# Fill products in the tensor engine's waits at the end of part A, and one in place of six ahead of the second B chunk

## The chip, the cores and the metric

The kernel runs on one core of a Trainium2 chip. The metric is device time in microseconds (us) of one execution. TensorE (PE) does the products, VectorE (DVE) and ScalarE (ACT) the copies and the softmax, GpSimd (POOL) copies inside SBUF and passes semaphores on, SyncE (SP) issues nearly all DMA transfers.

## The reference

Two attention decode steps with one query per batch row, put side by side in the output. Part A has 32 query heads on 8 key/value heads and looks only at the last 2048 positions. Part B has 32 heads of its own and looks at all 8192.

```
q = (x @ wq) -> [4, 32, 1, 128]
A: k, v = cache[:, :, Sk - W:, :], each shared by 4 heads;   W = 2048
B: k, v = cache, whole;                                      Sk = 8192
p = softmax(q . k * 128**-0.5);  o = (p . v) @ wo
out = concat([A, B], axis=-1)                # 4 x 1 x 1024, bf16
```

Nearly all the bytes are the B caches: 4 x 32 x 8192 x 128 values of two bytes, twice, which is 537 MB of the 587 MB that are read.

## The kernel before

Work is cut into chunks. Part A has 8 chunks (`NCA`), one for each key/value head, with 2 MB of keys and 2 MB of values each. Part B has 32 chunks, four heads of one batch row each, with 8 MB of keys and 8 MB of values.

Keys arrive with positions on partitions, so PE transposes them in tiles of 128 x 128, eight tiles a group, into the PSUM tile `tr` (`emit_T`, recorded at L499). DVE or ACT copies a group to `kt` (L572, L570), and PE forms the scores of a group with products of up to 64 columns into `sc` (`emit_S`; nearly all plain products are recorded at L501). After the statistics and the exponentials, PE multiplies the weights with the values into `po` and, for the second half of a B chunk, into a part of `tr` (`emit_pv`). The output projection accumulates in `fin`.

Each engine runs a list of operations in a fixed order, written out by the code; waits are on counters of the other engines. SP's list is the order of the transfers: wq, the A chunks, then for each B chunk k and v (a B k transfer is issued at L408, a B v transfer at L447, A's keys and values at L378). A transfer waits until the place it writes is free: k of the next chunk until the transposes of the first half of this chunk's keys are done, v until the products of the chunk before have read their half of the values. POOL passes the landing of each B transfer on to PE (`land_kB`, `land_vB`) and copies the second half of each k into a spare place (L423), which starts when that k has landed.

The end of part A is `finish_A`. It works off what is left of the last A chunk, on PE in this order: the transpose of the row maxima (`gmax-1`), four small products that sort the outputs of the chunk before (`sel-2`), the broadcast of the maxima (`bc-1`), the 128 products that form part B's queries (`q_products(1)`), the sum for the norm (`norm-1`), 64 products with the last A values (`emit_pv`), and again four small products (`emit_sel`).

A B chunk is `whole_B`. On PE it begins with `reorder` (16 products of 512 columns on 32 rows), two products whose result nobody reads (`keep_busy`, `NBUSY = 2`), and `more_busy`, a loop of such products at L927: `MOREBUSY + 1 = 6` in the chunks 1 to 28 of part B and one in the chunks 0, 29, 30 and 31. The first groups of transposes come after it. Such products without a use are called fill products here. Another helper, `fill(n)` (L944), loops over n of them; it stands twice at the start of the kernel (`FILL = (6, 3)`), before and after the products that form part A's queries. Its moving operand is a part of `pba` that holds zeros, and it waits for POOL to have written `identb` and `pba`.

The lists of PE, DVE and ACT are searched for repeating stretches, and these are written as loops; `finish_A` lies outside them.

Of the kernel before, what the change touches and what calls it, by code (L numbers as in the profile page):

```python
# [34 lines left out]
MOREBUSY = 5  # L35
# [141 lines left out]
def bass_concat_heads__sliding_block_cached__mha_block_cached__decode_kernel(  # L177
# [6 lines left out]
    DO = A_wo.shape[1]  # L184
# [37 lines left out]
    sch = _Sched()  # L222
    with ExitStack() as es:
        block = es.enter_context(nc.Block())

        def sb(name, shape, dt):
            return es.enter_context(nc.sbuf_tensor(name, shape, dt))

        def ps(name, shape, dt):
            return es.enter_context(nc.psum_tensor(name, shape, dt))  # L230
# [10 lines left out]
        identb = sb("identb", [P, P], BF16)  # L241
# [23 lines left out]
        pbt = {0: sb("pba", [P, NPB, NTA * 16 + NW], BF16), 1: sb("pbb", [P, 2, NTB * 2 + NW], BF16)}  # L265
# [4 lines left out]
        sel4 = sb("sel4", [P, 4, P], BF16)  # L270
# [5 lines left out]
        sc = ps("sc", [P, 2, 512], F32)  # L276
# [15 lines left out]
            fill=0.0, base=0, channel_multiplier=-1), waits=["c_onesb"], key="c_identb")  # L292
# [4 lines left out]
            fill=0.0, base=0, channel_multiplier=-1), waits=["c_onesf"], key="c_identf")  # L297
# [4 lines left out]
            waits=["c_onesf", "c_identf"], key="c_ind")  # L302
# [14 lines left out]
        for r in range(4):  # L317
            sch.add("pool", lambda e, r=r: e.affine_select(
                out=sel4[:, r, :], in_=onesb[:, :], pattern=[[0, 4], [-4, 32]], compare_op=ALU.is_equal,
                fill=0.0, base=-r, channel_multiplier=1), waits=["c_onesb"], key="c_sel" if r == 3 else None)  # L320
# [3 lines left out]
        for u in range(4):  # L324
            sch.add("pool", lambda e, u=u: e.affine_select(
                out=back[:, :, :], in_=back[:, :, :], pattern=[[1, 4], [-1, P]], compare_op=ALU.not_equal,
                fill=1.0, base=-P * u, channel_multiplier=4), waits=["c_back0" if u == 0 else ("c_back", u - 1)], key=("c_back", u))
# [14 lines left out]
        def flat(at, n):  # L342
            return kv[:, at:at + n, :].rearrange("p s x -> p (s x)")
# [153 lines left out]
        def pe_mm(o, l, r, start=True, stop=True, transpose=False, waits=(), key=None):  # L497
            if transpose:
                sch.add("pe", lambda e: e.transpose(o, l, r), waits, key)  # L499
            else:  # L500
                sch.add("pe", lambda e: e.matmul(o, l, r, start=start, stop=stop), waits, key)  # L501
# [13 lines left out]
        def q_products(ab):  # L515
            wqr = flat(half_of[("wq", ab)], 2)
            for h in range(HQ):
                for r in range(KC):
                    last = h == HQ - 1 and r == KC - 1
                    pe_mm(ms[:, Q0 + h * NB: Q0 + (h + 1) * NB], wqr[:, (r * HQ + h) * P:(r * HQ + h + 1) * P],  # L520
                          xT[:, ab, r * NB:(r + 1) * NB], start=r == 0, stop=r == KC - 1,
                          waits=[("wq", ab), "xT"] + ms_read if h == r == 0 else [],
                          key=("qmm", ab) if last else None)

        def q_out(ab):
            src = ms[:, Q0:Q0 + HQ * NB]
            dst = qs[:, ab * NB * HQ:(ab + 1) * NB * HQ]
            if ab == 1:

                src, dst = src.rearrange("p (hq u b) -> p hq b u", b=NB, u=4), dst.rearrange("p (hq b u) -> p hq b u", b=NB, u=4)  # L530
            else:
                src, dst = src.rearrange("p (g c b) -> p g b c", b=NB, c=REP), dst.rearrange("p (g b c) -> p g b c", b=NB, c=REP)
            sch.add("dve", lambda e: e.tensor_copy(dst, src), waits=[("qmm", ab), "c_qs"], key=("q", ab))
            ms_read[:] = [("q", ab)]
# [206 lines left out]
        def emit_pv(c, g):  # L741
            ch = chunks[c]
            UC = ch["UC"]
            half = NTB // 2
            for t in range(TG):
                j = g * TG + t
                if c < NCA:
                    base = 16 * (c % NSM)
                    waits = [("exp", c)] + po_read + [("v", c)] if j == 0 else []
                    if j == 0:  # L750
                        po_read[:] = []
                    pe_mm(po[:, base:base + NW], tile_of("v", c, j), pbt[0][:, par(c), j * UC:j * UC + NW],
                          start=j == 0, stop=j == ch["NT"] - 1, waits=waits, key=("pv", c) if j == ch["NT"] - 1 else None)
                    continue
                h, jj = j // half, j % half
                waits = [("exp", c, h)] + (po_read if h == 0 else []) if jj == 0 else []
                if j == 0:
                    po_read[:] = []
                waits += [("vr", c, g)] if t == 0 and g in QV else []
                o = (po2 if h else po)[:, 0:NW]  # L760
                pe_mm(o, tile_of("v", c, j), pbt[1][:, h, jj * 4:jj * 4 + NW], start=jj == 0, stop=jj == half - 1,
                      waits=waits, key=("pv", c, h) if jj == half - 1 else None)
# [35 lines left out]
        def norm_out(c):  # L798
            if c < NCA:
                m = c % NSM  # L800
                o, i0, i1 = oT[:, m, :], po[:, m * 16:m * 16 + 16], rinv[:, m, :]
                waits = [("rinv", c), ("pv", c)] + ([("sm", c - 2)] if c >= 2 else [])
            else:

                o, i0 = oz[:, :].rearrange("p (b u) -> p b u", b=NB), bcast(po2[:, 0:4], [[0, NB], [1, 4]])
                i1 = rz[:, :].rearrange("p (b u) -> p b u", b=NB)
                waits = [("rz", c), ("pv", c, 1)] + ([("fin", c - 1)] if c > NCA else ["c_oz"])
            sch.add("dve", lambda e: e.tensor_tensor(out=o, in0=i0, in1=i1, op=ALU.mult), waits=waits, key=("oT", c))
            if c < NCA:
                po_read[:] = [("oT", c)]  # L810
# [14 lines left out]
        def reord_at(u):  # L825
            return po[:, :] if u == 3 else tr[:, u, :].bitcast(F32)
# [51 lines left out]
        def do_A(what, c):  # L878
            name, n = what.split("-")
            c -= int(n)  # L880
            if c < 0:
                return
            {"gmax": stats_gmax, "bc": stats_bc, "shift": shift_A, "exp": exp_A, "sums": sums_A, "norm": norm_sum,
             "spread": lambda c: spread_A(c, range(4)), "spread01": lambda c: spread_A(c, (0, 1)), "spread23": lambda c: spread_A(c, (2, 3)),
             "sel": emit_sel, "fin": emit_fin}[name](c)
# [36 lines left out]
        def more_busy(c):  # L922

            n = c - NCA

            def mm(e):
                return e.matmul(sc[:, 1, :], identb[:, :], sel4[:, :, :].rearrange("p r x -> p (r x)"), start=True, stop=True)  # L927

            def emit(e, x=0):
                if isinstance(e, _Record):  # L930
                    return mm(e)
                if isinstance(x, int):
                    mm(e)
                    return None
                with nc.Fori(0, (((x + n + 31) >> 5) - ((x + n + 3) >> 5)) * MOREBUSY + 1, 1, engines=type(mybir.ALL_ENGINES)([mybir.EngineType.PE])):
                    mm(e)
                return None

            sch.add("pe", emit, at=n)

        def fill(n):

            def mm(e):
                return e.matmul(sc[:, 1, :], identb[:, :], pbt[0][:, 1, 0:DO], start=True, stop=True)  # L944

            def emit(e):
                if isinstance(e, _Record):
                    return mm(e)
                with nc.Fori(0, n, 1, engines=type(mybir.ALL_ENGINES)([mybir.EngineType.PE])):
                    mm(e)  # L950
                return None

            sch.add("pe", emit, waits=["c_identb", ("c_pb", 0)])

        def whole_B(c):

# [41 lines left out]
            emit_fin(c)  # L998

        def finish_A():  # L1000
            for what in ['gmax-1', 'sel-2', 'bc-1', 'shift-1', 'exp-1']:
                do_A(what, NCA)
            q_products(1)
            for what in ['spread-1', 'sums-1']:
                do_A(what, NCA)
            q_out(1)
            sch.relay("act", sems, "eng_sp", 1, [("q", 1)])
            do_A('norm-1', NCA)
            for g in range(chunks[NCA - 1]["NG"]):
                emit_pv(NCA - 1, g)  # L1010
            norm_out(NCA - 1)
            emit_sel(NCA - 1)

        emit_xT()
        fill(FILL[0])
        q_products(0)
        q_out(0)
        fill(FILL[1])
        emit_qb(0)
        for c in range(NCA):  # L1020
# [3 lines left out]
            values_A(c - 1 if c else None, c)  # L1024
        sch.mark()
        finish_A()
        for c in range(NCA, NC):
            whole_B(c)
# [67 lines left out]
```

## Time and profile before

| | us |
|---|---|
| median of 3 runs | 1373.03 (1371.73 to 1373.15) |
| the profiled execution, its own time | 1370.3 |
| its span, first to last instruction | 1368.6 |
| PE busy | 1230.5 (90%) |
| PE weight loads busy | 1125.3 (82%) |
| DVE busy | 731.5 (53%) |
| ACT busy | 555.5 (41%) |
| POOL busy | 210.1 (15%) |
| mean granted TensorE clock | 0.974 |

All times inside an execution count from the start of its span. A row of the timeline gives the start, the length, engine, line, operation, the tiles (out<-in) and the number of instructions; in square brackets stands how long the engine was idle before the row and what ended that. A row of the windows view gives for a stretch its length, then busy time and count for PE, PE's weight loads, DVE, ACT and POOL, then the granted TensorE clock (1.00 is full), the busy share of the 16 DMA engines and the GB/s they moved. A share a little over 1 in a short stretch comes from whole packets being counted in it.

### The profile page before, as it was taken

Reading aid. Unit: us, or ns where it says so; the run is one execution under the profiler, and the core shown is the slowest. Engines: PE = TensorE matmul, PEld = TensorE weight load, DVE = VectorE, ACT = ScalarE, POOL = GpSimd, SP = SyncE. Lnnn points to the kernel's source line nnn. Section 1 sums busy time; section 2 is a strip of 40 time slices with the busy share of each in tenths; the row PEclk is TensorE's granted clock in tenths of the full one; section 3 lists DMA queues with packets and bytes.
Section 4 is the critical chain, followed back from the end, with each engine's and each line's share of the span. In section 5 each row is a group of like instructions: output and inputs, shape, how many; then the busy total and the mean of one; then the engine's idle time right before and its main releaser. Section 6 shows DMA issues by size and latency. Waiting matters only on the chain.

```text
span 1368.6 us, 62991 instructions
## 1 busy us (share of the span) xinstructions
PE 1230.5 (90%) x27848; PEld 1125.3 (82%) x27848; DVE 731.5 (53%) x1495; ACT 555.5 (41%) x777; POOL 210.1 (15%) x86
## 2 busy tenths in 40 slices
PE   6868799988988999989989999898999898989998
PEld 5767688888887988878889888888888888878888
DVE  3655355554554555545545555454555554546555
ACT  3533244433444443434344434333444343434444
POOL 2000022222210222222101222221012222210000
PEclk9988999999999999999999999999999999999999
DMA  9999999999999999999999999999999999999998
GB/s 399 429 426 429 432 435 431 425 433 429 429 437 437 429 429 431 442 429 429 439 433 431 431 435 441 439 421 433 444 433 423 437 439 435 429 433 435 420 432 349
DMA packets 16053, 587.52 MB, mean 429 GB/s; under 512 B 1800, under 2 KB 1824, under 8 KB 3872
## 3 DMA queue, kind: packets, MB, share of 16 engines
q1 hardware_dynamic: 16000, 587.21, 99.6%
q8 instruction: 15, 0.25, 0.1%
q14 instruction: 6, 0.05, 0.0%
q10 hardware_dynamic: 32, 0.01, 0.0%
HBM read 587.21 MB, written 0.01 MB: 429 GB/s over the span
## 4 chain that ended last, share of the span: by engine, by line
DMA 50%; PE 44%; issue 2%; DVE 2%; ACT 1%; ACTq 0%; SPq 0%; POOLq 0%; DVEq 0%
DMA kv<-in_B_k_cache_dram 47%; PE tr L499 24%; PE sc L501 11%; PE tr L501 4%; DMA kv<-in_A_k_cache_dram 3%; PE po L501 2%; PE ms L501 1%; DMA kv<-in_A_wq_dram 1%; PE sc L927 1%; PE fin L501 1%; DVE kt L572 1%; ACT pbb L694 1%; DVE sA L625 0%; PE ms L499 0%; ACT pba L724 0%
## 5 line engine op out<-in xcount | busy, mean ns | idle before, releaser
L499 PE MATMUL tr<-identb,kv 128*128 128x128 bf16 x8704 | 670.7, 223 | 47.8 <-POOLq L80 35.3
L572 DVE COPY kt<-tr 128x1024 bf16<-128x1024 bf16 x736 | 502.5, 690 | 319.9 <-PE tr L499 316.5
L499 PEld LDWEIGHTS tr<-identb,kv 128*128 128x128 bf16 x8704 | 520.0, 100 | 60.5 <-issue 46.5
L570 ACT ACTIVATE kt<-tr 128x1024 bf16<-128x1024 bf16 x352 | 359.6, 1024 | 457.8 <-PE tr L499 455.6
L501 PE MATMUL sc<-qq,kt 128*128 128x64 bf16 x8192 | 400.9, 192 | 11.3 <-DVE kt L572 9.4
L423 POOL COPY kv<-kv 128x4096 int32<-128x4096 int32 x56 | 200.2, 3604 | 1021.1 <-DMA kv<-in_B_k_cache_dram 1021.1
L501 PEld LDWEIGHTS sc<-qq,kt 128*128 128x128 bf16 x8192 | 330.7, 98 | 17.9 <-DVE kt L572 12.7
L694 ACT ACTIVATE pbb<-sc,negb 32x128 bf16<-32x128 f32 x256 | 138.1, 540 | 133.6 <-DVE negb L676 130.8
L501 PE MATMUL tr<-pbb,kv 128*128 128x64 bf16 x4096 | 135.6, 193 | 29.0 <-ACT pbb L694 25.6
L501 PEld LDWEIGHTS tr<-pbb,kv 128*128 128x128 bf16 x4096 | 131.0, 99 | 32.7 <-issue 32.7
L501 PE MATMUL po<-pbb,kv 128*128 128x64 bf16 x4096 | 133.8, 193 | 1.0 <-issue 1.0
L501 PEld LDWEIGHTS po<-pbb,kv 128*128 128x128 bf16 x4096 | 126.3, 98 | 2.1 <-issue 1.1
L842 ACT ACTIVATE wol<-tr 128x512 bf16<-128x512 f32 x32 | 19.1, 597 | 202.2 <-PE po L501 202.2
L844 DVE CAST wol<-tr 128x512 bf16<-128x512 f32 x64 | 41.2, 685 | 56.1 <-PE tr L501 53.2
L927 PE MATMUL sc<-sel,identb 128*128 128x512 bf16 x172 | 53.3, 390 | 13.8 <-issue 13.8
L927 PEld LDWEIGHTS sc<-sel,identb 128*128 128x128 bf16 x172 | 17.0, 99 | 50.6 <-issue 40.7
L701 DVE TENSOR_REDUCE rs<-pbb 128x4 f32<-128x512 bf16 x32 | 21.9, 686 | 50.3 <-ACT pbb L694 50.3
L501 PE MATMUL tr<-wos,back 32*128 32x512 bf16 x384 | 35.7, 390 | 0.7 <-issue 0.5
L774 DVE RECIPROCAL ib<-ms 128x8 f32<-128x8 f32 x32 | 6.6, 208 | 53.3 <-PE ms L501 53.3
L501 PE MATMUL po<-wos,back 32*128 32x512 bf16 x128 | 34.7, 392 | 0.0
L662 DVE TENSOR_REDUCE gm<-ms 4x4 f32<-4x128 f32 x72 | 19.8, 274 | 25.2 <-PE ms L499 25.2
L642 DVE TENSOR_REDUCE rh<-sc 128x4 f32<-128x512 f32 x32 | 22.1, 691 | 14.3 <-PE sc L501 14.3
(90 smaller groups left out, 515.9 us busy)
## 6 DMA issues: line engine op xcount, KB each, us to landing
kv<-in_B_v_cache_dram SPq DMA_DIRECT2D x9, 4096.0 KB, 22.1
kv<-in_B_k_cache_dram SPq DMA_DIRECT2D x6, 4096.0 KB, 19.8
kv<-in_A_k_cache_dram SPq DMA_DIRECT2D x8, 2048.0 KB, 15.3
kv<-in_A_v_cache_dram SPq DMA_DIRECT2D x8, 2048.0 KB, 16.0
kv<-in_B_k_cache_dram SPq DMA_DIRECT2D x4, 2048.0 KB, 22.4
kv<-in_A_wq_dram SPq DMA_DIRECT2D x1, 4096.0 KB, 12.6
wor<-in_A_wo_dram SPq DMA_DIRECT2D x8, 512.0 KB, 22.1
kv<-in_B_wq_dram SPq DMA_DIRECT2D x1, 4096.0 KB, 17.4
```

What stands on the lines that cost most here:

```text
L423: sch.add("pool", lambda e, dst=dst, org=org: e.tensor_copy(dst, org), waits=[("T", s0 + ch["NG"] - 1)] if g == QC[0] else [])
L499: sch.add("pe", lambda e: e.transpose(o, l, r), waits, key)
L501: sch.add("pe", lambda e: e.matmul(o, l, r, start=start, stop=stop), waits, key)
L570: sch.add("act", lambda e: e.activation(dst, src, ACTF.Copy), waits=waits, key=("ev", s))
L572: sch.add("dve", lambda e: e.tensor_copy(dst, src), waits=waits, key=("ev", s))
L642: sch.add("dve", lambda e: e.tensor_reduce(out=dst, in_=src, axis=AX.X, op=ALU.max), waits=[("S", ch["s"] + (half + 1) * ch["NG"] // 2 - 1 ...
L662: sch.add("dve", lambda e: e.tensor_reduce(out=gm[0:C, m, 0:U], in_=src, axis=AX.X, op=ALU.max), waits=[key_of("trm", c, half)], key=key_o ...
L694: sch.add("act", lambda e, src=src, dst=dst, pp=pp, u=u: e.activation(dst, src, ACTF.Exp, bias=negb[pp, half, u:u + 1], scale=scale), wait ...
L701: sch.add("dve", lambda e: e.tensor_reduce(out=dst, in_=probs_of(c, half).rearrange("p j u -> p u j"), axis=AX.X, op=ALU.add), waits=[("ex ...
L842: sch.add("act", lambda e, u=u, o=o: e.activation(wol[:, u, :], o, ACTF.Copy), waits=[("reord", c, u)], key=("wol", c, u))
L844: sch.add("dve", lambda e, u=u, o=o: e.tensor_copy(wol[:, u, :], o), waits=[("reord", c, u)], key=("wol", c, u))
L927: return e.matmul(sc[:, 1, :], identb[:, :], sel4[:, :, :].rearrange("p r x -> p (r x)"), start=True, stop=True)
```

## The change

Three things change.

- `finish_A` gets four fill products in three loops: two ahead of `gmax-1`, one ahead of `bc-1`, and one between `q_products(1)` and the sum for the norm. They write `reord_at(0)`, the first bank of `tr`.
- `more_busy` runs one fill product in place of six in chunk 1, the second B chunk. All other chunks keep their number.
- `fill` takes an output as a second argument, and its moving operand is now `sel4`, the selection matrix that `more_busy` streams too; it waits for `sel4` instead of `pba`. This holds for the two old places as well.

```
-                with nc.Fori(0, (((x + n + 31) >> 5) - ((x + n + 3) >> 5)) * MOREBUSY + 1, 1, ...):
+                with nc.Fori(0, (((x + n + 30) >> 5) - ((x + n + 3) >> 5)) * MOREBUSY + 1, 1, ...):
                     mm(e)
...
-        def fill(n):
+        def fill(n, at=None):
             def mm(e):
-                return e.matmul(sc[:, 1, :], identb[:, :], pbt[0][:, 1, 0:DO], start=True, stop=True)
+                return e.matmul(sc[:, 1, :] if at is None else at, identb[:, :],
+                                sel4[:, :, :].rearrange("p r x -> p (r x)"), start=True, stop=True)
...
-            sch.add("pe", emit, waits=["c_identb", ("c_pb", 0)])
+            sch.add("pe", emit, waits=["c_identb", "c_sel"])
...
         def finish_A():
-            for what in ['gmax-1', 'sel-2', 'bc-1', 'shift-1', 'exp-1']:
+            for n, what in zip((2, 0, 1, 0, 0), ('gmax-1', 'sel-2', 'bc-1', 'shift-1', 'exp-1')):
+                if n:
+                    fill(n, reord_at(0))
                 do_A(what, NCA)
             q_products(1)
+            fill(1, reord_at(0))
             for what in ['spread-1', 'sums-1']:
                 do_A(what, NCA)
```

More of the change, by code (lines that the diff above doesn't have):

```diff
@@ L934, in emit @@
                     return None
-                with nc.Fori(0, (((x + n + 31) >> 5) - ((x + n + 3) >> 5)) * MOREBUSY + 1, 1, engines=type(mybir.ALL_ENGINES)([mybir.EngineType.PE])):
+                with nc.Fori(0, (((x + n + 30) >> 5) - ((x + n + 3) >> 5)) * MOREBUSY + 1, 1, engines=type(mybir.ALL_ENGINES)([mybir.EngineType.PE])):
                     mm(e)
@@ L939, in more_busy @@
             sch.add("pe", emit, at=n)
-        def fill(n):
+        def fill(n, at=None):
             def mm(e):
-                return e.matmul(sc[:, 1, :], identb[:, :], pbt[0][:, 1, 0:DO], start=True, stop=True)
+                return e.matmul(sc[:, 1, :] if at is None else at, identb[:, :], sel4[:, :, :].rearrange("p r x -> p (r x)"), start=True, stop=True)
             def emit(e):
```

## The prediction

> **What bounds the kernel now.** I read the page first: the row of DMA shares, the bytes and the chain that ended last.
>
> ```profile
> span 1368.6 us, 62991 instructions
> ...
> DMA  9999999999999999999999999999999999999998
> ...
> HBM read 587.21 MB, written 0.01 MB: 429 GB/s over the span
> ...
> DMA 50%; PE 44%; issue 2%; DVE 2%; ACT 1%; ACTq 0%; SPq 0%; POOLq 0%; DVEq 0%
> ```
>
> The transfers fill the span. PE takes nearly half of the chain as well, so the question is whether PE ever makes a transfer start too late. POOL's timeline answers it, because its first copy in a chunk starts when that chunk's k has landed and PE has finished the chunk before.
>
> ```profile
> 171.57 7.14 POOL L423 COPY kv<-kv 128x4096 int32<-128x4096 int32 x2 [160.06 <-DMA kv<-in_B_k_cache_dram]
> 210.32 7.15 POOL L423 COPY kv<-kv 128x4096 int32<-128x4096 int32 x2 [31.61 <-DMA kv<-in_B_k_cache_dram]
> 249.09 7.15 POOL L423 COPY kv<-kv 128x4096 int32<-128x4096 int32 x2 [31.62 <-DMA kv<-in_B_k_cache_dram]
> 289.07 7.15 POOL L423 COPY kv<-kv 128x4096 int32<-128x4096 int32 x2 [32.83 <-DMA kv<-in_B_k_cache_dram]
> 327.79 7.15 POOL L423 COPY kv<-kv 128x4096 int32<-128x4096 int32 x2 [31.56 <-DMA kv<-in_B_k_cache_dram]
> ```
>
> The k of B chunks 1 to 5 land 38.75, 38.77, 39.98 and 38.72 us apart. Between two stand 16.78 MB (8 MB of v, 8 MB of k; the third distance also holds 0.52 MB of wo, 1.2 us). That is 433 MB per ms each time. The first distances, where PE is still late, are as short as the last, where PE waits for the data. So from 171.57 us on the transfers lose nothing to PE. SP's timeline shows why: each transfer is issued before the one ahead of it has landed.
>
> ```profile
> 122.11 0.80 SPq L447 DMA_DIRECT2D kv<-in_B_v_cache_dram  x2
> ...
> 160.79 8.56 SPq L447 DMA_DIRECT2D kv<-in_B_v_cache_dram  x2
> 185.53 0.33 SPq L408 DMA_DIRECT2D kv<-in_B_k_cache_dram  x1
> 202.29 5.49 SPq L447 DMA_DIRECT2D kv<-in_B_v_cache_dram  x2
> ...
> 244.76 0.33 SPq L447 DMA_DIRECT2D kv<-in_B_v_cache_dram  x1
> ```
>
> 8 MB take 38.72 / 2 = 19.4 us. Slack, landing ahead minus issue: v of chunk 0, 171.57 - 38.7 - 122.11 = 10.8; first half of v 1, 171.57 - 160.79 = 10.8; k 2, 171.57 + 19.4 - 185.53 = 5.4; v 2, 210.32 - 202.29 = 8.0; v 3, 249.09 - 244.76 = 4.3. The least is 4.3 us. PE may be later than now by that much before the end moves, and being earlier moves nothing behind 171.57.
>
> What can be won lies ahead of it. The last A chunk's k landed at 87.20 + 13.26 = 100.46.
>
> ```profile
> 87.20 13.26 DMA kv<-in_A_k_cache_dram
> ```
>
> From there to 171.57 are 71.1 us for two A v (2.1 MB each), 0.52 MB of wo and three 8 MB transfers, 29.9 MB, which at the steady 433 take 69.0. So 2.1 us at most are lost there, to whatever cause, and this is the ceiling of any gain through earlier transfers in this execution.
>
> **The change part by part.** PE at the end of part A and at the start of part B:
>
> ```profile
> 108.57 1.56 PE L501 MATMUL po<-pba,kv 128*128 128x64 bf16 x48
> ...
> 111.49 0.27 PE L499 MATMUL ms<-identf,rm 128*4 128x128 f32 x1 [1.35 <-DVE rm L637]
> ...
> 113.20 0.58 PE L501 MATMUL ms<-identf,gx 4*128 4x4 f32 x2 [0.81 <-DVE zA L821]
> ...
> 114.13 3.55 PE L501 MATMUL ms<-xT,kv 128*128 128x4 bf16 x128 [0.35 <-DVE negb L680]
> ...
> 118.06 0.60 PE L501 MATMUL ms<-rsa,onesf 128*128 128x16 f32 x2 [0.38 <-DVE qs L533]
> ...
> 118.51 3.57 PE L501 MATMUL po<-pba,kv 128*128 128x64 bf16 x64
> ...
> 123.19 0.63 PE L501 MATMUL tr<-wos,back 32*128 32x512 bf16 x3 [0.50 <-issue]
> ...
> 126.31 1.77 PE L499 MATMUL tr<-identb,kv 128*128 128x128 bf16 x24
> ```
>
> *The four fills.* A fill of the same shape runs in the kernel now:
>
> ```profile
> 172.95 2.30 PE L927 MATMUL sc<-sel,identb 128*128 128x512 bf16 x6
> ...
> 175.09 1.50 PE L499 MATMUL tr<-identb,kv 128*128 128x128 bf16 x24
> ```
>
> Six from 172.95 to 175.09 are 0.36 us each. Two stand in the 1.35 us wait for the row maximum (0.72, fits), one in the 0.81 us wait ahead of `bc` (fits), one in the 0.38 us wait ahead of the norm (0.36; at worst it pushes the 64 value products by its own length). Nothing queued behind them is late; I cost them at 0 (between 0 and 0.4 us on PE). If the idle time went away they would cost 4 x 0.36 = 1.4 us of PE, within the slack.
>
> *What the fills may do: the clock.* The windows view, cut into stretches of 3.41 us that end at the falls and rises of the granted clock:
>
> ```profile
> 109.79:113.20 3.41, 0.87 (x17) 0.47 (x13) 2.95 (x11) 0.00 (x0) 0.00 (x0) 1.00 1.07 452
> 113.20:116.61 3.41, 3.06 (x95) 3.01 (x96) 1.18 (x4) 2.10 (x5) 0.00 (x0) 0.50 0.99 423
> ...
> 120.03:123.44 3.41, 2.58 (x47) 2.28 (x48) 0.84 (x5) 0.00 (x0) 0.00 (x0) 0.50 0.98 418
> 123.44:126.85 3.41, 3.41 (x25) 1.40 (x18) 1.30 (x3) 1.08 (x2) 0.00 (x0) 0.50 0.98 418
> ...
> 137.09:140.50 3.41, 2.03 (x49) 2.02 (x49) 1.37 (x2) 0.32 (x2) 0.00 (x0) 1.00 0.97 413
> 143.92:147.33 3.41, 1.46 (x29) 1.33 (x27) 0.87 (x3) 0.17 (x1) 0.00 (x0) 1.00 1.03 442
> ```
>
> The clock halves behind a stretch with 0.87 us of PE work and behind one with 1.46 (43%); it stays behind 2.03 (59%). It comes back only behind one that is full; 3.06 did not do. With three fills the stretch from 109.79 has 0.87 + 3 x 0.36 = 1.95 us, 57%: probably, not surely, enough. If the clock stays, the 64 value products go at the pace of the 48 at 108.57 (1.56 / 48 = 32.5 ns each instead of 55.8: -1.5 us). From reorder to the first transposes now pass 126.31 - 123.19 = 3.12 us. At full clock:
>
> ```profile
> 208.30 0.41 PE L501 MATMUL tr<-wos,back 32*128 32x512 bf16 x3
> ...
> 209.31 0.60 PE L501 MATMUL sc<-sel,identb 128*128 128x512 bf16 x2
> 209.75 1.03 PE L927 MATMUL sc<-sel,identb 128*128 128x512 bf16 x4
> ```
>
> 208.30 to 209.75 and one fill of 0.36 make 1.8 us: -1.3. The 128 query products have no full-clock row; between 0 and half of 3.55 us, I take 0, as four columns leave little to stream. The sum is 1.5 + 1.3 = 2.8 us earlier at B's first transposes (ends 0, if the clock falls all the same, and 4.6). [...]
>
> [...]
>
> *Chunk 1 with one fill.* Five fewer save 5 x 0.36 = 1.8 us of PE. But its k lands at 171.57 and its transposes start at 175.09, so at most 3.5 us of all this shows in chunk 1; what PE gains beyond that becomes a wait for k 1, and with one fill in it the clock can fall there: a half-speed stretch or two, 1.7 us each, paid from the same 3.5. PE's later chunks inherit 0 to 3.5 us and then wait for k 2 or k 3. What is late next is always a k. End of the kernel: 0.
>
> *The new operand.* `fill` at the start waits for `sel4` instead of `pba`:
>
> ```profile
> 6.71 1.09 POOL L318 TENSOR_SCALAR_AFFINE_SELECT sel<-onesb 128x128 bf16<-128x128 bf16 x4
> ...
> 8.05 0.39 PE L499 MATMUL ms<-identb,xs 4*128 4x4 bf16 x8 [8.05 <-DMA xs<-in_B_x_dram]
> 8.38 2.74 PE L944 MATMUL sc<-pba,identb 128*128 128x512 bf16 x6
> ```
>
> `sel4` is done at 7.80, and PE gets to the fill at 8.38, held by x until 8.05: 0. If x came early, PE would wait until 7.80, and the query products behind the fills wait for wq in any case.
>
> *SP and POOL* get nothing added and no order changed. v 0 is issued up to 1.5 us earlier, as the value products it waits for end earlier. It stood 10.8 us ahead of need, but the 16 engines do not end together, and part of the 2.1 us may be theirs. Between 0 and 2.1 I take 0.5 us.
>
> The sum is 1370.3 - 0.5 = 1369.8 for the profiled execution. That lies 2.7 us under the median of the runs, 1373.03; I apply the difference to the median: 1372.5.
>
> **The rivals.** *Faster by over 0.2%.* The executions without a profile lose 2.7 us more than this one. If that is PE's lateness (where the free stretches of the clock happen to be cut differs from run to run), v 3 or k 2 would be late there, and the change regains it with the 2.1: 1373.03 - 2.7 - 2.1 = 1368.2 at best, half of it for a middle, 1370. For it: v 3's slack is only 4.3. Against: no distance between k's shows any loss here. It decides from 4.3 us of lateness on.
>
> *The fills don't hold the clock.* 57% lies just above 43%, the query products behind them may not count as work, and 3.06 us of such a stretch did not bring the clock back. Then PE is as late as before, 1373.0, no change. [...]
>
> *Slower by over 0.2%: PE runs out of code.* In B's first pass PE stops inside groups of products, with no data to wait for:
>
> ```profile
> 145.94 0.32 PE L501 MATMUL sc<-qq,kt 128*128 128x64 bf16 x5 [1.95 <-issue]
> ...
> 166.54 1.61 PE L501 MATMUL tr<-pbb,kv 128*128 128x64 bf16 x46 [3.41 <-issue]
> ```
>
> These gaps lie in code that is met for the first time. Three more loops ahead move where they fall, and a PE that comes 2.8 us earlier meets them more. Two more of 3.41 us, with a half-speed stretch (1.7 us) behind each, make 10.2 us; less the 2.8 and the 4.3 of slack, +3.1: 1376.1. Against: three loops are few instructions beside a chunk's. It decides from 4.3 us of net lateness.
>
> **How the numbers follow.** About 0.2%, 2.7 us, is what a measurement of this kernel can tell from no change. No change, with the clock held (0.40) or not (0.30): 0.70. Faster: 0.17. Slower: 0.13. The likeliest time is 1372.5. The range runs from 1369.6 (the 2.1 and half of the 2.7) to 1375.6 (most of the rival's +3.1); both outer cases keep about half of their chance outside, 0.15 in all.
>
> **What would show it.** Right: the distances between k landings stay 38.7; clock 1.00 from 113 to 123; first B transposes near 123.5; chunk 1's transposes start behind 171.6, released by the landing; v 3 issued earlier than 244.76. Wrong: a k distance under 38.7 in after, which would mean that before had lost transfers to PE; a k 1 landing more than 2 us off 171.6; new issue gaps in B's first chunk and a v issued behind the landing ahead of it. The end would stay: after the last packets (the share falls to 0.08 in the stretch below) only the last products and the output are left.
>
> ```profile
> 1363.00:1364.00 1.00, 1.00 (x40) 1.00 (x36) 0.44 (x3) 0.00 (x0) 0.00 (x0) 1.00 0.08 33
> ```

## The result, and the profile after

| | before | after |
|---|---|---|
| median of 22 runs each, side by side, us | 1371.09 (1369.49 to 1374.44) | 1375.05 (1371.23 to 1378.21) |
| ratio to before | | 1.0027 [1.0019, 1.0034] |
| the profiled execution, its own time, us | 1370.3 | 1376.4 |
| its span, us | 1368.6 | 1374.6 |

The change makes the kernel slower, by 0.27% or 3.7 us (0.0027 x 1371.09). The times of after spread more widely than those of before: 10 of the 22 lie from 1371.2 to 1373.9, and 12 from 1374.8 to 1378.2. The profiled execution is one of the longer ones; no trace of a shorter one was taken.

The page of after: span, DMA share in 40 slices, the queue that brings the engines' instructions, and the chain that ended last.

```profile
span 1374.6 us, 62984 instructions
...
DMA  9999899999999999999999999999999999999998
...
q8 instruction: 16, 0.26, 0.1%
...
DMA 57%; PE 37%; issue 2%; DVE 2%; ACT 1%; SPq 0%; ACTq 0%; POOLq 0%; DVEq 0%
```

The bytes read are the same (587.21 MB), so the 6.0 us more are time in which the transfers stood. The fifth slice (137 to 172 us) shows an 8 where before had a 9. The instruction queue carried 16 packets, one more than in before, whose page has:

```profile
q8 instruction: 15, 0.25, 0.1%
```

What that packet did shows in PE's timeline of after, from the end of part A to B's first transposes, and then at the values of B's chunk 0.

```profile
111.17 0.27 PE L499 MATMUL ms<-identf,rm 128*4 128x128 f32 x1 [0.88 <-DVE rm L637]
...
113.62 3.49 PE L501 MATMUL ms<-xT,kv 128*128 128x4 bf16 x128 [0.35 <-DVE negb L680]
116.97 0.59 PE L944 MATMUL tr<-sel,identb 128*128 128x512 bf16 x1
...
117.94 3.56 PE L501 MATMUL po<-pba,kv 128*128 128x64 bf16 x64
121.84 0.26 PE L501 MATMUL ms<-oT,sel 128*128 128x16 bf16 x4 [0.34 <-DVE oT L808]
128.86 0.63 PE L501 MATMUL tr<-wos,back 32*128 32x512 bf16 x3 [6.76 <-issue]
...
131.98 2.76 PE L499 MATMUL tr<-identb,kv 128*128 128x128 bf16 x24
...
168.71 2.85 PE L501 MATMUL po<-pbb,kv 128*128 128x64 bf16 x50 [4.58 <-issue]
```

Ahead of `reorder`, B's first operation, PE stands 6.76 us without any data to wait for; in before it stood 0.50. B's first transposes start at 131.98, 5.7 us later. Some 40 us later a second such gap, 4.58 us, lies inside the products of chunk 0's weights with the first half of its values. SP waits for those products before it issues the first half of chunk 1's values.

```profile
121.53 0.80 SPq L447 DMA_DIRECT2D kv<-in_B_v_cache_dram  x2
171.59 5.01 SPq L447 DMA_DIRECT2D kv<-in_B_v_cache_dram  x2
...
252.29 0.33 SPq L447 DMA_DIRECT2D kv<-in_B_v_cache_dram  x1
```

The issue at 171.59 stood at 160.79 before. The 10.8 us are the late start, the longer gap (4.58 where before's at the same products was 1.00) and 1.2 us of half clock in these 50 products (2.85 us instead of 1.63); 6.0 + 3.6 + 1.2 = 10.8, where 6.0 is the distance of the first of these products, 161.17 against 155.16. Only the late start is surely the change's: the gap inside the values is 3.76 us with chunk 1 alone, where the code up to there is that of before, and 4.86 with one loop alone, two kernels below that lose nothing. Two rows of before, left out in the prediction, carry the sum:

```profile
155.16 1.33 PE L501 MATMUL po<-pbb,kv 128*128 128x64 bf16 x40
...
159.12 1.63 PE L501 MATMUL po<-pbb,kv 128*128 128x64 bf16 x50 [1.00 <-issue]
```

The landings of k, by POOL's first copies in after, and the windows view around the first of them (length, busy time and count of PE, its weight loads, DVE, ACT and POOL, granted clock, DMA share, GB/s):

```profile
171.25 7.14 POOL L423 COPY kv<-kv 128x4096 int32<-128x4096 int32 x2 [159.76 <-DMA kv<-in_B_k_cache_dram]
215.09 7.15 POOL L423 COPY kv<-kv 128x4096 int32<-128x4096 int32 x2 [36.71 <-PE tr L501]
253.84 7.14 POOL L423 COPY kv<-kv 128x4096 int32<-128x4096 int32 x2 [31.60 <-DMA kv<-in_B_k_cache_dram]
295.19 7.15 POOL L423 COPY kv<-kv 128x4096 int32<-128x4096 int32 x2 [34.20 <-DMA kv<-in_B_k_cache_dram]
```

```profile
166.00:170.00 4.00, 1.29 (x25) 1.29 (x26) 0.92 (x3) 0.57 (x3) 0.00 (x0) 0.50 0.34 139
170.00:174.00 4.00, 4.00 (x102) 4.00 (x100) 0.00 (x0) 0.00 (x0) 2.75 (x1) 0.68 0.45 131
```

The distances are 43.8, 38.8 and 41.3 us, where before had 38.8, 38.8 and 40.0: 5.0 us are lost behind k 1 and 1.3 behind k 3, together 6.3; the span grew by 6.0. Such a distance counts only the last of the 16 DMA engines. In bytes the loss lies nearly all around k 1's landing: the windows view of 166 to 176 us has 206 GB/s where before has 401, that of 176 to 200 us has 416 against 445, and at 433 this is 4.5 + 1.6 = 6.1 us. So the 1.3 behind k 3 is hardly a loss of its own. The engines run dry from ahead of the landing on: in the eight microseconds around 170 they are idle for 4 x (1 - 0.34) + 4 x (1 - 0.45) = 4.8 us, as some of them have finished their part of k 1 while others have not, and nothing is queued. In the trace's records the sixteen ends of k 1 lie between 167.4 and 171.0 us.

### The profile page after: what moved, and what is told of

The parts are those of the page before. It is cut to its first block, busy times and chain, and to the rows that moved or that the text cites. A ratio compares the mean times of both kernels' runs of the same rounds, so it can differ in the third digit from the quotient of the medians.

```text
span 1374.6 us, 62984 instructions
## 1 busy us (share of the span) xinstructions
PE 1232.6 (90%) x27847; PEld 1127.9 (82%) x27847; DVE 734.7 (53%) x1495; ACT 555.0 (40%) x777; POOL 210.0 (15%) x86
## 3 DMA queue, kind: packets, MB, share of 16 engines
q1 hardware_dynamic: 16000, 587.21, 99.2%
HBM read 587.21 MB, written 0.01 MB: 427 GB/s over the span
## 4 chain that ended last, share of the span: by engine, by line
DMA 57%; PE 37%; issue 2%; DVE 2%; ACT 1%; SPq 0%; ACTq 0%; POOLq 0%; DVEq 0%
DMA kv<-in_B_k_cache_dram 52%; PE tr L499 22%; PE sc L501 10%; DMA kv<-in_A_k_cache_dram 2%; PE tr L501 2%; DMA kv<-in_B_v_cache_dram 2%; PE po L501 2%; PE ms L501 1%; DMA kv<-in_A_wq_dram 1%; DVE sA L625 0%; PE fin L501 0%; DVE kt L572 0%; ACT pbb L694 0%; PE sc L927 0%; DVE rz L779 0%
## 5 line engine op out<-in xcount | busy, mean ns | idle before, releaser
L501 PEld LDWEIGHTS tr<-wos,back 32*128 32x128 bf16 x384 | 14.1, 94 | 19.8 <-issue 15.9
```

## The experiments

Five theories were put against each other. B: the branches of the three new loops cost the time, however short the loops are. L is B in its strictest form: the loop right ahead of `norm-1` alone is enough. S: any added instruction shifts the code against the blocks in which it is fetched, and that costs. C: the one fill in chunk 1 costs the time. E, formed after the first four runs: the code ahead of B's loop is a few instructions longer, runs over into one more block of instructions, and PE has to wait for the block behind it.

A block is 256 instructions here: in B's first pass PE's waits without data end 512, 768, 1280 and 1536 instructions behind the loop's head in before (at 138.47, 145.94, 159.12 and 166.54 us, waits of 1.94, 1.95, 1.00 and 3.41) and 512, 768, 1024 and 1280 behind it in after (at 143.61, 150.80, 159.15 and 168.71 us, waits of 0.29, 1.68, 0.97 and 4.58), counted in the records of both traces. Every packet of the instruction queue (q8) has 16384 bytes there, and each of these waits ends 2.3 to 2.6 us behind the start of one.

In the code, the head of PE's B loop is bound to the first slot of a block (`loop_on(mybir.EngineType.PE, (None, 0))`, the 0), so the code ahead of it ends somewhere inside a block and the rest of that block is jumped over; the trace of before has this jump at 122.5 us, and it takes 0.40 us there. If that code runs over the block's end, a few instructions stand alone in one more block. Each plain product is two instructions of PE (weights and product), each fill loop five (in the trace a move, the product's two, an arithmetic one and a branch), so the change adds 15 ahead of the loop. One goes: before has an instruction that waits on a semaphore ahead of `gmax-1`, at 109.7 us, and in after the first loop's move carries that wait. So the net growth is 14.

**The same fills without loops** (8 instructions, net 7).

```
-                if n:
-                    fill(n, reord_at(0))
+                straight(n)       # n plain products, written out
...
-            fill(1, reord_at(0))
+            straight(1)
```

> The changed kernel with the four fill products of finish_A written one after the other, not as loops. Theory L (the branch of the loop behind the query products makes PE fetch the next block of code anew, so that PE stands without code ahead of B's first reorder): the gap ahead of the first reorder falls from 6.8 us to under 1.5 us, the first B transposes start near 126, the k of chunks 1 and 2 land 38.8 us apart, and the time is that of the kernel before within 0.2%. Rival S (any added instruction shifts the code against the blocks in which it is fetched; 8 are added here, 12 in the change): the gap stays above 4 us and the time stays about 4 us over before. Rival C (one fill in place of six lets chunk 1 fall behind): still about 4 us slower than before, with no gap ahead of reorder.

Measured: 1371.18 us, 1.0004 [0.9994, 1.0013]. The gap is not there, and the instruction queue has 15 packets. PE's timeline of this kernel:

```profile
122.73 0.63 PE L501 MATMUL tr<-wos,back 32*128 32x512 bf16 x3 [0.50 <-issue]
```

The fill products as such cost nothing. S falls, as the code is shifted and no gap comes; its expectation counts four instructions for a loop, where the trace has five. E and B both allow this result: the branches are gone and the code is shorter.

**One loop alone** (5 instructions): `zip((0, 0, 0, 0, 0), ...)`, so that only the loop ahead of `norm-1` is left.

> The changed kernel with only the fill loop between the query products and the norm in finish_A; the loops ahead of gmax and bc are left out. Theory L: this one loop is enough, a gap of 5 to 7 us ahead of the first reorder in most executions, the time 3 to 5 us over before. Rival S: 4 instructions of shift, a smaller gap or none, time within 0.2% of before. Rival C: about 4 us slower without a gap.

Measured: 1371.26 us, 1.0002 [0.9992, 1.0012], gap 0.50, 15 packets. L falls. PE's timeline at the values of chunk 0:

```profile
159.14 2.85 PE L501 MATMUL po<-pbb,kv 128*128 128x64 bf16 x50 [4.86 <-issue]
```

The second gap and the half clock behind it are here too, and nothing is lost: k 1 and k 2 land 38.8 us apart.

**Two loops** (10 instructions, net 9): the line `fill(1, reord_at(0))` behind the query products is taken out.

> The changed kernel without the fill loop between the query products and the norm; the three fills ahead of gmax and bc stay as loops. Theory L: no gap over 1.5 us ahead of the first reorder, the time of before within 0.2%. Rival S: 8 instructions of shift, the gap stays and the time is 3 to 5 us over before. Rival C: about 4 us slower without a gap.

Measured: 1370.18 us, 0.9995 [0.9985, 1.0005], gap 0.50, 15 packets.

**Chunk 1 alone**: before, with only the count of `more_busy` changed.

```
-  nc.Fori(0, (((x + n + 31) >> 5) - ((x + n + 3) >> 5)) * MOREBUSY + 1, 1, ...):
+  nc.Fori(0, (((x + n + 30) >> 5) - ((x + n + 3) >> 5)) * MOREBUSY + 1, 1, ...):
```

> The kernel before with only the count of fill products changed: one in place of six in the second B chunk. Theory L and rival S: no added code, so no gap ahead of the first reorder and the time of before within 0.2%. Rival C: about 4 us slower, chunk 1's clock at half at the start of its transposes, and v of chunk 2 or k of chunk 2 issued behind the landing ahead of it.

Measured: 1370.81 us, 0.9993 [0.998, 1.0007], gap 0.50. C falls: this part of the change costs nothing.

**Length without loops and without fills** (16 instructions): before, with eight products of four columns behind the query products.

```
             q_products(1)
+            for _ in range(8):
+                pe_mm(reord_at(0)[:, 0:4], identb[:, :], sel4[:, 0, 0:4], ...)
```

> The kernel before with 8 products of 4 columns (16 instructions with their weight loads, some 0.2 us of PE) written straight behind the query products in finish_A; no fill, no loop, chunk 1 as before. Theory E (the code ahead of the B loop now ends a few instructions behind the end of a fetch block of 256; the loop starts at the head of the next block, whose fetch is only asked for when PE enters the short piece, so PE stands for the whole fetch): a gap of 5 to 8 us ahead of the first reorder, one more packet on the instruction queue (16), the time 3 to 5 us over before in half of the executions or more. Rival B (it takes the branches of three loops): no gap, 15 packets, the time of before within 0.2%.

Measured: 1378.13 us (1373.89 to 1379.64), 1.0038 [1.0018, 1.0057], 16 packets. The profiled execution is the shortest of its ten. PE's timeline:

```profile
122.17 0.39 PE L501 MATMUL ms<-oT,sel 128*128 128x16 bf16 x4 [0.34 <-DVE oT L808]
128.90 0.63 PE L501 MATMUL tr<-wos,back 32*128 32x512 bf16 x3 [6.33 <-issue]
```

The gap is back at the same place, with no loop added, and with it the loss. E holds and B falls. The step lies between 9 net instructions that fit and 14 that don't: in before the code ahead of the loop ends 9 to 13 instructions before a block's end.

**The change whole, with five instructions taken out elsewhere**: the second `fill(FILL[1])` at the start of the kernel, some 100 us ahead, is left out, so that the net growth is 9.

> The changed kernel, all four fills in finish_A as loops and one fill in chunk 1, without the second of the two fill loops at the start of the kernel (three products behind part A's query products, 5 instructions less ahead of the B loop). Theory E: the code fits its block again, no gap over 1.5 us ahead of the first reorder, 15 packets on the instruction queue, the time of before within 0.2%. Rival B: the gap stays and the time is 3 to 5 us over before.

Measured: 1370.82 us, 0.9982 [0.9964, 1.0001], gap 0.50, 15 packets. But the profiled execution was a long one, with a span of 1374.2 us and its losses spread over later chunks, and the interval was wide. So the same kernel was run again with more rounds:

> The changed kernel without the second fill loop at the start, the same kernel as no_start_fill, timed in more rounds: all that the change means to do, with the code ahead of the B loop inside its block. Prediction of the change without the fetch (transfers never wait for PE there): the time of before within 0.2%. Rival (the fills and the shorter chunk 1 win back part of the 2.1 us lost ahead of k 1): 1 to 2 us under before.

Measured: 1370.89 us in 12 runs, 0.9999 [0.9991, 1.0008], span 1367.7. Page and PE's timeline:

```profile
q8 instruction: 15, 0.25, 0.1%
```

```profile
122.46 0.41 PE L501 MATMUL tr<-wos,back 32*128 32x512 bf16 x3 [0.51 <-issue]
```

All that the change does to the work is in this kernel, and it takes the time of before.

**Delay alone, by fills in chunk 0.** The count of `more_busy` gets a term that adds 18 (or 10) passes in the first chunk only. The code ahead of the loop stays as it was.

```
+  ... * MOREBUSY + 1 + (1 - ((x + n + 31) >> 5)) * 18
```

> The kernel before with 18 fill products more in chunk 0's loop at the start of part B: PE is held for 18 x 0.43 = 7.7 us there. Slack as the prediction has it: the first half of v 1 is issued near 168.5 (10.8 us of slack, holds), k 2 near 193 against a landing ahead of it at 191, so 2 to 5 us are lost between the landings of k 1 and k 2 or k 2 and k 3, and the time is 2 to 5 us over before. Rival (only the missing code costs, lateness of PE is taken back elsewhere): the time of before within 0.2%.

> The kernel before with 10 fill products more in chunk 0's loop: PE is held for 4.3 us at the start of part B, no more than the least slack. Theory: all distances between landings of k stay at 38.8, the time of before within 0.2%. Rival (each us that PE loses ahead of chunk 1 moves the end by one): 4 us over before.

Measured: 1416.55 us, 1.0312 [1.0265, 1.036], and 1412.4 us, 1.0286 [1.0238, 1.0333]. Both failed as measurements of a delay: they lost 39 to 43 us, spread over all chunks. The first fence is PE's timeline of the kernel with 10 passes more, the second that of before, both at full clock in a later chunk.

```profile
302.15 0.39 PE L927 MATMUL sc<-sel,identb 128*128 128x512 bf16 x1 [0.51 <-issue]
303.05 0.39 PE L927 MATMUL sc<-sel,identb 128*128 128x512 bf16 x1 [0.51 <-issue]
```

```profile
365.24 0.39 PE L927 MATMUL sc<-sel,identb 128*128 128x512 bf16 x1 [0.24 <-issue]
365.87 0.39 PE L927 MATMUL sc<-sel,identb 128*128 128x512 bf16 x1 [0.24 <-issue]
```

One pass takes 0.90 us instead of 0.63: the longer expression for the count is paid at every pass, in each of the chunks that run six. In the trace five register and branch instructions stand between two passes instead of three. PE becomes the bound (with 10 passes more, most k landings behind the fifth are 39.1 to 41.5 us apart, where before has 38.7, and 40.0 in every fourth). They say nothing on the delay.

**A longer spill** (128 instructions): as the one with eight products, but with 64.

> The kernel before with 64 products of 4 columns (128 instructions, some 1.8 us of PE) written straight behind the query products in finish_A, no loop, chunk 1 as before. Theory E (the fetch of the loop's first block is asked for when PE enters the last block ahead of it): PE now runs some 115 instructions, about 3.3 us of value products, in that last block, so the gap ahead of the first reorder shrinks from 6.3 to 6.8 us to between 2.5 and 4.5 us; 16 packets on the instruction queue. Rival (any code past the block's end costs a fixed wait): 6 to 7 us. The time is 1 to 5 us over before, as the pads themselves hold PE too.

Measured: 1375.52 us, 1.0028 [1.0016, 1.0039], 16 packets, one fetch more as with eight. PE's timeline:

```profile
119.23 0.64 PE L501 MATMUL po<-pba,kv 128*128 128x64 bf16 x9
121.17 3.09 PE L501 MATMUL po<-pba,kv 128*128 128x64 bf16 x55 [1.30 <-issue]
...
127.79 0.63 PE L501 MATMUL tr<-wos,back 32*128 32x512 bf16 x3 [2.92 <-issue]
```

This run separates two mechanisms, a fixed wait and a fetch that runs beside PE's work. The block's end now falls inside the value products (gap of 1.30), PE enters the extra block at 121.17, works in it, and still waits 2.92 us at its end. Behind this entry stand 119 of the instructions ahead of the loop (55 products, 54 weight loads, the eight of the sorting products, a move and the jump), so 9 of the 128 added ones fit and in before exactly 9 slots were free; the change's 14 run over by five. From the entry into the extra block to the loop's first instruction pass 6.62 us, about as many as where PE has nearly nothing to do in that block (the gap alone is 6.76 in after, 6.33 with eight products). So the block behind seems to be asked for when PE enters the one ahead of it, and at this place it came 6.3 to 6.8 us later, with PE at work meanwhile or not. The records of the instruction queue's packets agree: the packet of the loop's block starts at 125.0 us here, at 126.1 in after and with eight products, 3.8 to 4.3 us behind the entry (121.2, about 121.8 and 122.3). The jump to the loop's head does not ask for it: it is at 124.7 here, 0.3 us ahead of the packet, and 4.2 us ahead of it in after. Counted from the end of the packet before it the distance is 5.3 to 6.5 us, which fits less well but is not ruled out.

**A delay of the right kind**: the kernel with one loop alone (5 instructions, which fit), that loop with 11 and with 19 passes in place of one. The count is a constant, and a pass costs 0.33 us (the products behind the loop start 8.06 us behind the query products with 11 passes and 10.67 with 19).

> The kernel third_only with 11 passes in place of one in the fill loop behind the query products: no added instruction, PE held for 10 x 0.38 to 0.43, about 4 us, ahead of part B. Theory of the lead (a v half has to be issued about 5 us ahead of the landing of the k in front of it, not just ahead of it, since 2.3 us of lead lost 2.5 us in pad8 and none lost 5.0 in the change): the first half of v 1 is issued near 165 to 166, 5 to 6 us ahead of k 1's landing near 171, so 0 to 1 us is lost. The prediction's plain slack: nothing lost, within 0.2% of before. Rival (every us of lateness moves the end): 4 us over before.

> The same loop with 19 passes: PE held for about 7.3 us, as long as the change's gap holds it, with the code fetched in time. Theory of the lead: the first half of v 1 is issued near 168 to 170, 1 to 3 us ahead of k 1's landing, and 2 to 4 us are lost between the landings of k 1 and k 2; the time is 2 to 5 us over before, as with the change. Rival (only missing code costs, lateness does not): the time of before within 0.2%. The prediction's plain slack of 10.8 us for v 1 and 5.4 us for k 2: 0 to 2 us over before.

Measured: 1370.37 us, 0.9999 [0.9986, 1.0013] with 11, and 1372.07 us, 1.0005 [0.9994, 1.0016] with 19. SP's and POOL's timelines of the profiled execution with 19, whose own time was 1375.2 us, the second longest of its ten:

```profile
167.19 6.22 SPq L447 DMA_DIRECT2D kv<-in_B_v_cache_dram  x2
```

```profile
171.27 7.14 POOL L423 COPY kv<-kv 128x4096 int32<-128x4096 int32 x2 [159.78 <-DMA kv<-in_B_k_cache_dram]
212.29 7.14 POOL L423 COPY kv<-kv 128x4096 int32<-128x4096 int32 x2 [33.88 <-DMA kv<-in_B_k_cache_dram]
```

No gap ahead of `reorder`, and still 2.3 us lost behind k 1 (41.0 instead of 38.75), although v 1 was issued 4.1 us ahead of that landing. That is the lateness acting by itself. Set side by side, the profiled executions give the lead that a transfer needs (issue of v 1 ahead of the landing of k 1, and what was lost up to k 2):

| kernel | v 1 issued, us | k 1 landed, us | lead, us | lost, us |
|---|---|---|---|---|
| before | 160.79 | 171.57 | 10.8 | 0 |
| one loop, 11 passes | 164.44 | 171.35 | 6.9 | 0 |
| one loop, 19 passes | 167.19 | 171.27 | 4.1 | 2.3 |
| eight products | 169.00 | 171.29 | 2.3 | 2.5 |
| after | 171.59 | 171.25 | -0.3 | 5.0 |

The median of the kernel with 19 passes doesn't stand off from before, where 2 to 5 us over it were expected, so a start 5 us late (`reorder` at 127.78 against 122.61 with one pass) is about where losses begin.

**The head of the loop alone**: the change whole, with the slot of the loop's head as the one edit, first 64, then free.

```
-  sch.emit_looped("pe", e, sems, loop_on(mybir.EngineType.PE, (None, 0)))
+  sch.emit_looped("pe", e, sems, loop_on(mybir.EngineType.PE, (None, 64)))      # then (None, None)
```

> The changed kernel with one argument changed: the head of PE's B loop is placed at slot 64 of a fetch block and not at slot 0. The code ahead of it is the change's. Theory E: the spilled instructions and the loop's head now lie in the same block, whose fetch is asked for when PE enters the block ahead, at the end of the query products; the gap ahead of the first reorder falls from 6.8 us to under 2 us and the time is that of before within 0.2%. Rival (code that spills past the block costs its fetch wherever the loop begins): the gap stays at 6 to 7 us, the time 3 to 5 us over before. Gaps inside B's first pass move, as the body's block ends do.

> The changed kernel with the head of PE's B loop not placed at all, so that the loop follows the code ahead of it. Theory E: as head64, the gap ahead of the first reorder under 2 us, the time of before within 0.2%, unless the unplaced loop costs in every chunk (a distance between k landings over 38.8). Rival: the gap stays at 6 to 7 us.

Measured: 1370.74 us, 1.0002 [0.9992, 1.0011], and 1370.27 us, 0.9998 [0.9988, 1.0007]; 15 packets each. PE's timeline with slot 64:

```profile
122.79 0.63 PE L501 MATMUL tr<-wos,back 32*128 32x512 bf16 x3 [0.40 <-issue]
```

Every instruction of the change is in these two kernels, and neither gap nor loss is. None of the versions is measurably faster than before.

## Why the prediction was right or wrong

**The forecast was wrong in its sign.** It took 1372.5 us and no change, with 0.13 for slower; measured are 1375.05 us and slower, inside the stated range (1369.6 to 1375.6) but at its end. That it lies inside is luck: the forecast started from a median of three runs, 1373.03, while before measures 1371.09 side by side, and from there the same sum gives 1370.6.

**The step that failed is the weighing of the third rival**, "PE runs out of code". Its place, PE's code at first sight, was right, and its +3.1 us is near the measured 3.7. What failed is the sentence against it, "three loops are few instructions beside a chunk's". It is not the number of instructions that counts but where the last one falls: 9 more fit, 14 don't, and the five that run over cost a whole fetch. The prediction named neither the head bound to a block, which stands in the code, nor where the code ahead of it ends. The price was also put together otherwise than it came: two more gaps of 3.41 us were assumed; it was one new gap of 6.76 ahead of the loop, and a gap in chunk 0's values of 4.58 in place of 1.00, which is as long with one loop alone, where nothing is lost. So the nearness of the price is luck.

**The slack was overstated.** The step "slack, landing ahead minus issue" made 10.8 us for the first half of v 1, 4.3 for v 3, and said that PE may be 4.3 us later before the end moves. The landing is the end of the last of 16 engines, and the first are idle well before: in the traces of the table k 1's first end is at 167.4 to 167.6 us, and counted to it the five leads are 6.6, 3.0, 0.4, -1.6 and -4.2 us. A lead of 6.9 us lost nothing and one of 4.1 lost 2.3, so of v 1's 10.8 between 4 and 7 were free. For v 3 a lead of 4.3 (before) lost nothing and 1.55 (after: issued 252.29, landing 253.84) lost 1.3 by the distance, though hardly anything in bytes. The bound of lateness, 4.3 us, came out near where losses begin, but through the wrong transfer.

**The gain term was wrong: these fills did not hold the clock.** The prediction gave 2.8 us for it and 57% as "probably, not surely, enough". The windows view of after, cut at its own fall and rise of the clock:

```profile
111.14:114.55 3.41, 2.07 (x46) 1.53 (x47) 2.09 (x11) 0.55 (x2) 0.00 (x0) 1.00 1.02 432
114.55:117.97 3.42, 3.42 (x101) 2.98 (x98) 0.75 (x3) 1.67 (x5) 0.00 (x0) 0.50 1.00 426
117.97:121.38 3.41, 3.41 (x65) 3.39 (x65) 0.26 (x1) 0.10 (x1) 0.00 (x0) 0.50 1.12 471
```

A stretch with 2.07 us of PE work (61%) is followed by half clock. About 0.9 of the 2.07 are the first of the query products (from 113.62 on), and the next stretch, filled with them for 2.6 us, does not bring the clock back, while the one behind it, filled with products of 64 columns, does. So the four-column products seem not to count as work; without them the first stretch has 1.1 us, 33%, and belongs with the 43% that fell in before. In each of the ten traces in which the fall was read it came between 112.0 and 116.4 us, with the fills and without; in two executions of the same kernel, the change without the second `fill`, it came at 116.4 and at 114.0. This was the prediction's second rival, "the query products behind them may not count as work", and it held; its time, "as late as before", would have been the result without the spill. "It comes back only behind one that is full" is true of the prediction's rows alone: later in before the clock comes back behind a stretch with 2.87 us of PE work (1068.93 to 1072.34), less than the 3.06 that did not do, of which some 2.5 were query products.

**What held.** The transfers are the bound, and what moves the time is a transfer issued too late. Chunk 1 with one fill costs 0 (0.9993). The new operand and the fills' own time on PE cost 0 (0.9999 for the change without the spill). The 128 query products have no gain from a full clock: 3.49 us in after, mostly at half clock, and 3.43 in the first run without the second `fill`, where the clock stayed full for their first 1.9 us, so the 0 taken for them was right. Of what was to show the forecast wrong, "new issue gaps in B's first chunk and a v issued behind the landing ahead of it" is what came, the first of them just ahead of that chunk.

**Open.** Why 10 of after's 22 runs show little or no loss was not traced. With losses that set in between 4 and 7 us of lead and a fetch that takes 6.3 to 6.8 us, a part of the runs may just escape; that is argued, not shown. Nor was it settled how the later gaps of B's first pass fall out: the one inside chunk 0's values was 1.00 us in before, 4.86 with one loop alone and 5.13 with 19 passes, all without a spill, and 4.31 to 4.58 in the three kernels with one. A run of after with a short gap there would issue v 1 some 4 us earlier; whether the shorter times are such runs is not shown.

## What to carry to other kernels

Count the instructions ahead of a loop whose head is bound to a block of code, and see how many are free up to the block's end: an edit that runs over by a few can pay a whole fetch, even if its work is free (here five instructions over the end, and a wait of 6.76 us). Before trusting a slack of the kind "landing ahead minus issue", take off what the spread of the DMA engines eats, here between 4 and 7 us of 10.8. And when an edit of no work costs time, pad the old kernel to the new one's length, and move the loop's head in the new one: two runs separate the code's place from the code's work.

## What the runs showed of the hardware

- At the head of PE's B loop the fetch of a block of instructions, with the DMA engines full (their share is 1.00 from 121.84 to 128.86 us in after), took 6.3 to 6.8 us from PE's entry into the block ahead, and the 64 products (6.62 us with PE at work) say that it is asked for at about this entry. As a wait it showed in full, 6.76 us, where PE had almost nothing to do in the block it was in, and with 2.92 us where PE had 3.7 us of work there. Inside B's first pass, from the end of one wait without data to the end of the next one block on, it varied more: 7.5 and 7.4 us in before, 7.2, 8.4 and 9.6 us in after, and from 6.1 (148.14 to 154.20) to 10.1 us (154.20 to 164.31) in the kernel with 19 passes.
- A block is 256 instructions and comes as one packet: the waits in B's first pass end at multiples of 256 instructions behind the loop's head (512 to 1536 in before, 512 to 1280 in after) and 2.3 to 2.6 us behind the start of a packet, each packet of the instruction queue (q8) has 16384 bytes, and the one block more in after is one packet more (16 against 15).
- The count of a loop that is worked out from registers is paid at each pass: 0.90 us (302.15 to 303.05 in the kernel with 10 passes more) instead of 0.63 (365.24 to 365.87 in before), with five register and branch instructions between two passes instead of three.
- 128 products with four columns took 3.55 us at half clock (before) and 3.43 us where the clock was full for the first 1.9 us, and a stretch of 3.4 us with 2.6 us of them didn't raise the clock.
- The 16 DMA engines end one transfer of 8 MB some microseconds apart (k 1 in after: 167.4 to 171.0 us): with nothing queued behind it, their mean share was 0.34 in the four microseconds ahead of the landing.
